# Fetching the second batch's first queries and keys earlier, and finishing the last tile in two halves

## The chip, the cores and the metric

One core of one Trainium2 chip. The time is the device time of one execution in microseconds (us). Every kernel was checked against the reference. A run counts as slow when it is over 1.5% above the fastest run of its kernel. All ratios compare fast runs alone; a median stands with all runs of its group.

## The reference

```python
# q, k, v: [4 batches, 8 heads, 768, 64]; mem_k, mem_v: [4, 8, 8, 64]; w1: [512, 2048]; w2: [2048, 512]
for c in range(768 // 32):                      # chunks of 32 queries, context 16 left and 8 right
    k_full = concat(mem_k, k[l_start:r_end])
    a = softmax(q[c] @ k_full.T / 8)
    attn[c] = a @ concat(mem_v, v[l_start:r_end])
x = attn.transpose(0, 2, 1, 3).reshape(4, 768, 512)
u = x + real(fft(fft(x, axis=1), axis=2))
un = (u - mean(u)) / sqrt(var(u) + 1e-6)
out = u + relu(un @ w1) @ w2
```

## The kernel before: the parts that matter

A batch is four "pairs" of heads: pairs 0 to 3 are the first batch, 4 to 7 the second, and so on. Each pair needs its query and key (loaded by GpSimd), its values (loaded by SyncE, then partly copied by GpSimd), transpositions, scores, exponentials, and the products with the values. Then come a batch's Fourier stage, its normalisation and the two large products (L669 with the first weights, L683 with the second).

```python
    def e_load_q(n):                            # L312; e_load_k (L317) alike
        b, pr = seq[n]
        nc.gpsimd.dma_start(qf[n % NS], q[b, 2 * pr:2 * pr + 2].rearrange(...))
    def e_overlap(n, hh):                       # L341, "the copies" of pair n
        v1 = va_at(n)[:, hh]
        nc.gpsimd.tensor_copy(v1[0:32, 1:NB, 0:D + 1], v1[96:128, 0:NT, 0:D + 1])
    # L439, the products with the values: 24 small matmuls in the trace for each half of a pair
    # L462, warm: matmuls of zeros that fill TensorE's holes
```

No engine runs in the order of the source. The kernel lists tasks, each with an engine, an estimated cost, what it comes after, and a rank; a small greedy planner walks through estimated time and places the first task that is ready, for every engine. "SPARE" gives margins, one row for each batch: the time by which what a task waits for must be done before the task may be placed. The order so found is fixed when the kernel is built.

```python
    SPARE = [(0.0, 0.0, 0.0), (1.5, 0.7, 2.0)] + [(1.0, 0.3, 0.5)] * (B - 2)
    def attention(n):
        b, pr = seq[n]
        behind1 = kept["ov"] if n == HP else None      # HP = 4: pair 4's query after the last copies of pair 3
        lq = add("POOL", 0.8, lambda: e_load_q(n), [behind1, kept.get("lk"), ...], take=("qf",), ...)
        lk = add("POOL", 0.8, lambda: e_load_k(n), [lq], take=("kf",), ...)
        mgp, mg, mgl = SPARE[b]
        ov = [add("POOL", 0.84, lambda hh=hh: e_overlap(n, hh), [lv[hh], calm], margin=mgl) for hh in range(2)]
        kept["ov"] = ov[-1]
        # ... transpositions, scores, exponentials, products with the values
    # ...
    with tc.manual_schedule():
        for plan.current in plan.order():
            plan.current["emit"]()
```

The softmax here doesn't subtract the row's maximum and nothing guards it: scores larger than these inputs give would overflow.

## Time and profile before

| | before |
|---|---|
| time, median of 3 (lowest to highest) | 308.03 us (307.89 to 308.85) |
| span of the profiled execution | 306.6 us, clock 0.999 |
| TensorE busy | 290.5 us, 95% |
| warm matmuls (zeros) | 170 |
| TensorE without work, 60 to 160 us | 6.3 us; 160 to 302 us: none |

TensorE is the bound, so time can only come from its holes and from the end. The profile's lines are in the prediction below.

### The profile page before, as it was taken

The page shows a single profiled execution, that of the slowest core. Times are in us where ns is not written, and L with a number is a line of the kernel's source. Part 1 is how long each engine was busy: PE and PEld are TensorE (multiplying, and loading weights), DVE is VectorE, ACT ScalarE, POOL GpSimd, SP SyncE. Part 2 cuts the span into 40 slices and gives each one's busy share as a digit, 9 for nine tenths or more (in the row PEclk, how much of TensorE's full clock was granted, in tenths as well). Part 3 has the DMA queues.
Part 4 walks back from the last instruction along what each step waited for, and adds up shares of the span by engine and source line. Part 5 has one row for each costly group of instructions (what it writes and reads, how often), then busy time and mean ns, then how long its engine had stood idle before and what let it go on. Part 6 is the DMA issues. An engine that isn't in the chain of part 4 may idle for free.

```text
span 306.6 us, 7853 instructions
## 1 busy us (share of the span) xinstructions
PE 290.5 (95%) x3335; PEld 193.2 (63%) x3335; DVE 177.6 (58%) x361; ACT 166.4 (54%) x297; POOL 72.7 (24%) x121
## 2 busy tenths in 40 slices
PE   8688999998999799997899999999999999999994
PEld 8577997666656476675566755767664554654641
DVE  7969968503525998699995989846911001001011
ACT  8967345887577556557475624641570450631710
POOL 7556837153336902223100020000010000000000
PEclk9999999999999999999999999999999999999999
DMA  6995999989996512323000010000000101102001
GB/s 81 151 174 116 190 199 197 198 140 154 206 194 119 95 40 61 94 57 92 2 0 2 2 71 35 2 34 34 36 0 34 72 0 68 36 0 90 15 34 68
DMA packets 42169, 24.49 MB, mean 80 GB/s; under 512 B 30359, under 2 KB 38551, under 8 KB 42135
## 3 DMA queue, kind: packets, MB, share of 16 engines
q0 software_dynamic: 9344, 10.49, 21.7%
q1 hardware_dynamic: 29335, 7.21, 13.0%
q10 hardware_dynamic: 3456, 6.29, 5.4%
q8 instruction: 26, 0.43, 0.6%
q14 instruction: 8, 0.07, 0.1%
HBM read 28.11 MB, written 6.29 MB: 112 GB/s over the span
## 4 chain that ended last, share of the span: by engine, by line
PE 84%; DVE 7%; ACT 6%; DMA 1%; issue 1%; POOL 0%; POOLq 0%; ACTq 0%
PE pc L683 27%; PE ph L669 26%; PE ps L513 9%; PE xa L439 6%; PE pm L548 5%; PE sc L384 2%; PE pm L612 2%; ACT e L427 2%; PE tp L648 1%; PE trq L348 1%; DMA qf<-in_q_dram 1%; PE trk L363 1%; PE warm L462 1%; ACT e L392 1%; ACT hT L676 1%; PE sc L417 1%
## 5 line engine op out<-in xcount | busy, mean ns | idle before, releaser
L676 ACT ACTIVATE hT<-ph 128x384 f16<-128x384 f32 x128 | 62.1, 491 | 60.0 <-PE ph L669 59.1
L669 PE MATMUL ph<-unT,w_sb 128*128 128x384 f16 x512 | 89.0, 326 | 3.4 <-ACT hT L676 1.7
L683 PE MATMUL pc<-w_sb,hT 128*128 128x512 f16 x384 | 89.0, 380 | 0.1
L669 PEld LDWEIGHTS <-w_sb 128*128 128x128 f16 x512 | 48.6, 98 | 35.5 <-issue 3.1
L689 DVE SCALAR_TENSOR_TENSOR osb<-pc,rstd,xsb 128x512 f32<-128x512 f32 x24 | 18.0, 750 | 75.5 <-PE pc L683 75.5
L683 PEld LDWEIGHTS <-hT 128*128 128x128 f16 x384 | 35.6, 98 | 39.3 <-issue 0.2
L341 POOL COPY va<-va 32x780 f32<-32x780 f32 x30 | 30.1, 1018 | 45.0 <-DMA va<-in_v_dram 43.9
L392 ACT ACTIVATE e<-sc,mbias 128x384 f32<-128x384 f32 x48 | 25.3, 582 | 9.1 <-PE sc L384 5.7
L439 PE MATMUL xa<-va,e 128*64 128x65 f32 x720 | 26.3, 225 | 0.0
L439 PEld LDWEIGHTS xa<-va,e 128*64 128x64 f32 x720 | 23.1, 137 | 4.1 <-issue 2.3
L642 ACT ACTIVATE un<-xsb,mu_s 128x512 f16<-128x512 f32 x18 | 13.0, 720 | 13.6 <-DVE mu_s L636 12.4
L660 POOL TENSOR_SCALAR rstd<-mu_s 128x6 f32<-128x6 f32 x4 | 1.0, 251 | 73.9 <-DVE mu_s L636 73.8
L450 DVE TENSOR_TENSOR xsb<-xa,zs 128x384 f32<-128x384 f32 x32 | 17.8, 557 | 1.1
L353 ACT COPY qT<-trq 128x768 bf16<-128x768 bf16 x14 | 11.2, 799 | 11.2 <-PE sc L384 11.2
L528 ACT CAST up<-ps 128x386 f16<-128x386 f32 x16 | 9.6, 603 | 13.5 <-PE ps L513 13.5
L635 DVE BATCH_NORM_STATS2 st<-xsb 128x6 f32<-128x512 f32 x24 | 16.5, 686 | 0.5
L449 DVE RECIPROCAL zs<-xa 128x6 f32<-128x6 f32 x32 | 6.1, 191 | 16.9 <-PE xa L439 16.5
L506 DVE TENSOR_TENSOR lo<-ff,hi 128x768 f16<-128x768 f32 x14 | 14.4, 1039 | 1.9 <-ACT hi L501 1.9
L501 ACT CAST hi<-ff 128x768 f16<-128x768 f32 x14 | 11.6, 830 | 7.1 <-DVE ff L594 4.7
L462 PE MATMUL warm<-zeros 128*128 128x128 bf16 x170 | 13.7, 245 | 1.0 <-DVE zero L249 1.0
L373 ACT COPY kTb<-trk 128x832 bf16<-128x832 bf16 x16 | 13.7, 858 | 1.4 <-PE sc L384 1.4
L629 DVE TENSOR_TENSOR xsb<-pm,xsb 128x512 f32<-128x512 f32 x18 | 12.1, 671 | 3.8 <-PE pm L548 3.8
(144 smaller groups left out, 400.9 us busy)
## 6 DMA issues: line engine op xcount, KB each, us to landing
out_dram<-osb ACTq DMA_DIRECT2D x24, 256.0 KB
va<-in_v_dram SPq DMA_DIRECT2D x30, 176.0 KB
w_sb<-in_moe_w_ch_dram POOLq DMA_DIRECT2D x8, 512.0 KB, 12.4
qf<-in_q_dram POOLq DMA_DIRECT2D x16, 192.0 KB, 5.3
kf_all<-in_k_dram POOLq DMA_DIRECT2D x16, 192.0 KB, 6.2
va<-in_mem_v_dram SPq DMA_DIRECT2D x30, 24.0 KB
va<-in_v_dram SPq DMA_DIRECT2D x15, 28.0 KB
last<-in_v_dram SPq DMA_DIRECT2D x2, 176.0 KB
```

Source lines behind the costliest of these rows:

```text
L341: nc.gpsimd.tensor_copy(v1[0:32, 1:NB, 0:D + 1], v1[96:128, 0:NT, 0:D + 1])
L392: nc.scalar.activation(e1[:, :, :, ts(half, 32)], sc[:, :, 0:6, ts(half, 32)], AFT.Exp, bias=mbias[:, half:half + 1], scale=1.0 / math.sqr ...
L439: nc.tensor.matmul(xa[64 * half:64 * half + 64, st, hh, 0:65], e1[:, hh, t6, :], v1[:, 6 * g + t6 + 1, 0:65], start=True, stop=True)
L450: nc.vector.tensor_tensor(xs[b][:, 3 * g:3 * g + 3, 2 * pr * D:(2 * pr + 2) * D] .rearrange("p s (h d) -> p s h d", h=2), xa[:, :, :, 0:D] ...
L462: nc.tensor.matmul(warm_of[0], zeros, zeros, start=True, stop=True)
L513: nc.tensor.matmul(out_[:, sp, :], part[:, ab, sp * 3 + st, c0:c1], tab[:, sp, st, :], start=(first and sp + st + i == 0), stop=(last and ...
L548: nc.tensor.matmul(pm[:, par, :], lhs, rhs[:, par, :], start=(im == 0), stop=(im == 3))
L635: nc.vector.bn_stats(st6, xs[b][:, kt, :])
L669: nc.tensor.matmul(ph[:, 0:384], w1_sb[:, dt, ts(ht, P)], unT_of[b][:, dt, sh * 384:(sh + 1) * 384], start=(dt == 0), stop=(dt == NDT - 1))
L676: nc.scalar.activation(hT_of[b, sh][:, ht, :], ph_of.pop((b, sh, ht))[:, 0:384], AFT.Relu, bias=0.0, scale=-1.0)
L683: nc.tensor.matmul(pc_of[b, sh, stl], hT_of[b, sh][:, ht, ts(stl, P)], w2_of[0][:, ht, :], start=(ht == 0), stop=(ht == NHT - 1))
L689: nc.vector.scalar_tensor_tensor(osb, pc_of.pop((b, sh, stl)), rstd_of[b][:, st:st + 1], xs[b][:, st, :], ALU.mult, ALU.add)
```

## The change

Intent: the queries and keys of pairs 4 and 5 are no longer fetched after the first batch's last copies, but between them, so that pair 4's transpositions and scores can fill holes of TensorE in the first batch's Fourier stage. At the end, the last tile's product is made in two halves of 256 columns, so that the last VectorE step and the last store are shorter. Pair 6's query, and so pair 7's, now comes behind the second weights.

```diff
     def attention(n):
         b, pr = seq[n]
-        behind1 = kept["ov"] if n == HP else None
+        behind1 = {HP: kept.get(("ov", 1)), HP + 1: kept.get(("ov", 2)),
+                   HP + 2: t_w2[-1] if n >= HP else None}.get(n)
 ...
-        kept["ov"] = ov[-1]
+        kept["ov"] = kept["ov", n] = ov[-1]
 ...
                 st = 3 * sh + stl
+                if (b, st) == (B - 1, NST - 1):
+                    for half in range(2):
+                        c2 = add("PE", 1.75, lambda half=half: e_ch2_half(half), ...)
+                        os_ = add("DVE", 0.42, lambda half=half: e_osb_half(half), [c2, rs], ...)
+                        add(("SP", "ACT")[half], 0.3, lambda half=half: e_out_half(half), [os_], ...)
+                    continue
```

More of the change, by code (lines that the diff above doesn't have):

```diff
@@ L684, in e_ch2, with e_ch2_half, e_osb_half, e_out_half @@
                              start=(ht == 0), stop=(ht == NHT - 1))
+    def e_ch2_half(half):
+        b, sh, stl = B - 1, 1, 2
+        pc_of[half] = bank([P, DM // 2], FP32, "pc_half")
+        for ht in range(NHT):
+            nc.tensor.matmul(pc_of[half], hT_of[b, sh][:, ht, ts(stl, P)],
+                             w2_of[0][:, ht, ts(half, DM // 2)],
+                             start=(ht == 0), stop=(ht == NHT - 1))
+    def e_osb_half(half):
+        b, st = B - 1, NST - 1
+        osb_of[half] = osb = fpool.tile([P, DM], FP32, tag="osb", bufs=3, name="osb")
+        cols = ts(half, DM // 2)
+        nc.vector.scalar_tensor_tensor(osb[:, 0:DM // 2], pc_of.pop(half),
+                                       rstd_of[b][:, st:st + 1], xs[b][:, st, cols],
+                                       ALU.mult, ALU.add)
+    def e_out_half(half):
+        eng = (nc.sync, nc.scalar)[half]
+        eng.dma_start(out[B - 1, ts(NST - 1, P), ts(half, DM // 2)],
+                      osb_of.pop(half)[:, 0:DM // 2])
     def e_osb(b, sh, stl):
@@ L1027, in mlp @@
                 st = 3 * sh + stl
+                if (b, st) == (B - 1, NST - 1):
+                    for half in range(2):
+                        c2 = add("PE", 1.75, lambda half=half: e_ch2_half(half),
+                                 [relu[-1], t_w2[-1], c2], take=("mlp",),
+                                 rank=MLPS + len(plan.tasks))
+                        os_ = add("DVE", 0.42, lambda half=half: e_osb_half(half), [c2, rs],
+                                  take=("osb",), give=(("mlp", c2),))
+                        add(("SP", "ACT")[half], 0.3, lambda half=half: e_out_half(half), [os_],
+                            give=("osb",), moved=0.5, rank=10 * MLPS)
+                    continue
                 for part in range(4):
```

## The prediction

> **What bounds the kernel now.** I read the page first (busy time, chain), then the table of windows, then the timeline around the two places that the diff touches, then the waits.
>
> ```profile
> PE 290.5 (95%) x3335; PEld 193.2 (63%) x3335; DVE 177.6 (58%) x361; ACT 166.4 (54%) x297; POOL 72.7 (24%) x121
> ...
> PE 84%; DVE 7%; ACT 6%; DMA 1%; issue 1%; POOL 0%; POOLq 0%; ACTq 0%
> ```
>
> TensorE is the bound: 84% of the chain that ended last. Its multiplications cannot shrink by this change, so the whole prize is the time in which TensorE waits or multiplies zeros to stay warm (L462). The table of windows says where it waits (span, then PE, PEld, DVE, ACT and POOL busy, clock, DMA share, GB/s):
>
> ```profile
> 20.00:30.00 10.00, 8.74 (x221) 7.60 (x221) 8.01 (x16) 6.99 (x12) 5.92 (x10) 1.00 0.62 115
> ...
> 60.00:70.00 10.00, 8.99 (x159) 6.05 (x156) 1.03 (x3) 9.10 (x18) 5.50 (x8) 1.00 0.95 150
> ...
> 100.00:110.00 10.00, 8.41 (x117) 5.44 (x113) 9.90 (x15) 6.13 (x11) 6.76 (x5) 1.00 0.36 65
> ...
> 140.00:150.00 10.00, 8.23 (x100) 5.34 (x99) 9.90 (x19) 7.78 (x14) 4.05 (x4) 1.00 0.25 66
> 150.00:160.00 10.00, 8.84 (x95) 6.63 (x94) 9.83 (x22) 5.75 (x11) 0.00 (x0) 1.00 0.01 2
> ```
>
> PE's missing time after 60 us is 1.0 (60 to 70), 0.2, 1.6 (100 to 110), 0.6 (130 to 140), 1.8 and 1.2 us: 6.3 us in all; from 160 to 302 us there is none. Where it misses most, VectorE is 98 to 99% busy. VectorE idles in 60 to 70 (1.03 us busy), and DMA has room in 20 to 30 (share 0.62, against 1.2 at 40 to 60). The lines of the timeline that the change turns on (start, duration, engine, line):
>
> ```profile
> 35.31 0.83 PE L462 MATMUL warm<-zeros 128*128 128x128 bf16 x12
> 38.00 0.50 PE L462 MATMUL warm<-zeros 128*128 128x128 bf16 x6
> 45.91 0.50 PE L462 MATMUL warm<-zeros 128*128 128x128 bf16 x6
> 65.43 0.35 PE L384 MATMUL sc<-qT,kTb 64*128 64x64 bf16 x12
> 43.72 0.63 POOL L317 DMA_DIRECT2D kf_all<-in_k_dram  x1 [2.02 <-DMA w_sb<-in_moe_w_ch_dram]
> 49.30 3.18 POOL L341 COPY va<-va 32x780 f32<-32x780 f32 x4
> 104.47 2.12 PE L669 MATMUL ph<-unT,w_sb 128*128 128x384 f16 x12 [1.59 <-DVE xsb L450]
> ```
>
> The warm matmuls fill holes during the first batch's Fourier stage; the second batch's first scores start only at 65.4 us, because its queries and keys queue behind the first weights (5.3 and 6.2 us median to landing, 15.6 and 14.9 at most). And the end:
>
> ```profile
> 302.33 0.75 DVE L689 SCALAR_TENSOR_TENSOR osb<-pc,rstd,xsb 128x512 f32<-128x512 f32 x1 [2.70 <-PE pc L683]
> 303.11 0.34 ACTq L693 DMA_DIRECT2D out_dram<-osb  x1
> ```
>
> **What the Trainium skill says.** "TensorE: Matmul & The Clock Gate", section "Wait — 56ns, not 53.3ns?", gives N / 2.4 GHz + about 2.5 ns between warm matmuls, 215.7 ns at N = 512. The trace agrees: 48 of L683 take 10.36 us in the chain, 215.8 ns each, and 48 of L548 (N = 256) take 5.24 us, 109.2 ns each. "DMA: Bandwidth & Descriptors", section "Anatomy of one DMA — SWDGE (gpsimd) path", says that a semaphore wait of a DMA happens on the issuing sequencer; the trace agrees, since GpSimd stands still 2.02 us before the key load at 43.72. "SBUF — State Buffer", section "SBUF: two separate sides", says that GpSimd and VectorE operations with two SBUF inputs lock each other out; the trace agrees: an addition of L481 takes 1.59 us beside the GpSimd copies at 99.7 us, 0.95 elsewhere.
>
> **The change part by part.** I compared the instruction orders of the two built kernels.
>
> (1) GpSimd now issues query and key of pair 4 (first of the second batch) after the copies of pair 1, and of pair 5 after those of pair 2: 2 x 1.4 us of issue (0.68 + 0.68 each) ahead of the last copies. Before, GpSimd is idle 2.3 us ahead of L585 at 27.43 us, waiting for VectorE. Working forward: copies of pair 1 end near 22.1, two issues to 23.5, copies of pair 2 (2.3 us in this trace) to 25.8, against 26.57 when TensorE's product needs them; two more issues to 27.2, when L585 can run at 27.4. It just fits. The bytes: four loads of 192 KB at some 195 GB/s are 4 us; the DMA shares of 22 to 29 us add up to about 3.3 of 7, so there is room, and I take up to 1 us of delay on the first weights.
>
> (2) TensorE: 18 warm matmuls disappear (170 become 152): 18 x 56 ns = **1.0 us**. In their place stand the 32 transpositions of pair 4 (0.34 + 0.37 us at the tightest rows of the chain) and its first 12 scores (0.35). Work leaves the bounded stretch and lands in a hole: -1.0 us on the path.
>
> (3) Scores and values of pairs 4 and 5 now come before and among the first L669 products instead of after 65 us. ScalarE and VectorE get their share of attention earlier, while VectorE idles, and value buffer 0 comes free some 15 us earlier. By my count of TensorE work the second batch's Fourier stage still begins after the same amount (93.1 before, 92.4 after), its columns come 4 us of work earlier and the third batch's rows 3 us later. So VectorE's crowded stretch is stretched a little. I expect about 1.5 of the 6.3 us of waits to go: the 1.0 of 60 to 70, and some of 140 to 152. This is the least certain term. **-1.5 us.**
>
> (4) A new wait. After the second weights GpSimd issues pairs 6, 7 and also 8 ahead of the copies (L341) of pair 4. Each GpSimd load waits for the one eight loads before it; for pair 8's key that is the second quarter of the second weights. Before, the first weights land near 43.7 us (the key load waited for them); a quarter is 512 KB, 2.7 us at 197 GB/s. So its landing is at 43.7 + 0 to 1 + 2 x 2.7 + 1 for value loads between, some 50.1 to 51.1; then 0.63 of issue and two copies of 0.84 end at 52.4 to 53.4. TensorE reaches the values of pair 4 at about 51.40 + 0.65 = 52.05, and the order puts them ahead of the first L669. **+0.8 us**, from 0 to 2.
>
> (5) The end. The last 16 matmuls of 512 become 2 x 16 of 256: 32 x 109.2 = 3.49 against 16 x 215.8 = 3.45 us, nothing. The last VectorE step halves: from 0.56 for 384 columns and 0.75 for 512 I estimate 0.38 for 256: -0.37. The last store falls from 256 to 128 KB; before, its bytes took about 0.65 us (0.96, 0.99, 0.58 of three quarter microseconds), so about -0.3; the first half leaves 1.75 us earlier on another queue. **-0.65 us.**
>
> Sum: -1.0 - 1.5 + 0.8 - 0.65 = -2.35, so 308.0 becomes about **305.7 us**.
>
> **The rivals.** (a) Nothing but the end moves: the weights, not queries and keys, pace the second batch. The DMA share is 1.2 from 44 to 64 us whatever the order, and the new wait (4) could take 2 us. For it: same bytes, full queues, and GpSimd's order of issue, so that copies stand behind weights. Against it: three holes are demonstrably filled by warm matmuls. Then 307 to 308.5.
> (b) VectorE becomes the bound in 94 to 160 us. It is 98 to 99% busy in four of those six windows, so earlier attention could free all waits there (6 us: 302) or none. For freeing: 26 us of VectorE idle in 60 to 100. Against: the count of TensorE work before the Fourier stage of the second batch is almost the same, so its rows cannot start much earlier. Then 303 to 304.
> (c) The early loads delay the first batch: values of pair 3 are issued at 21.2 to 24.1 us, beside query and key of pair 4, and the last copies need them at 27.7. If they land 2 us later, everything does. Against it: DMA is nearly idle at 26 to 28 us (shares 0.12 and 0.27). Then 308 to 310.
>
> **Range and chances.** The certain parts (2) and (5) are worth 1.65; (3) and (4) run from -3.5 to +1.5 together. That makes 303.3 to 308.0 as eight in ten. Two per cent is 6.2 us, about all of the waits after 60 us: faster 0.04. Slower by 6.2 needs rival (c) and a bad (4) together: 0.02. Within 2%: **0.94**.
>
> **What would show it.** Right: scores L384 first near 46 us instead of 65; 152 warm matmuls; PE idle below 0.5 us in 60 to 70; TensorE waiting up to 2 us for L341 or a product behind it near 52 us; the last store landing about 0.65 us sooner after the last matmul. Wrong: the first ps (L513, at 33.3 us) begins over 0.5 us later (rival c); or PE's idle time in 100 to 160 changes by over 2 us in either direction, which would say that (3), not (2), sets the result; or the L669 products of the first batch end as late in relation to the work done as before (rival a).

## The result, and the profile after

| | before | after |
|---|---|---|
| time, median (lowest to highest) | 308.21 us (307.89 to 308.85), 4 runs | 305.38 us over all 4 runs; 304.71 us (304.57 to 306.04) over the 3 fast ones; the fourth was slow, 309.99 at clock 0.983 |
| span of the profiled execution | 306.6 us | 304.2 us, clock 1.000 |
| warm matmuls | 170 | 152 |

The ratio is 0.9897, with a 95% interval of 0.9858 to 0.9935: within 2%. A ratio is the mean time of one kernel's fast runs over that of the other's of the same rounds, so not quite the ratio of the medians quoted. By this ratio and that of e1 (0.991) the gain is 2.8 to 3.2 us, where 2.35 was predicted: close. The profiled run was the slowest of the three fast ones. All outputs are right.

First the page of the changed kernel: busy time, then the chain, that is, the work that ended last, followed back step by step to what released it.

```profile
PE 290.3 (95%) x3333; PEld 193.2 (64%) x3333; DVE 179.2 (59%) x362; ACT 166.0 (55%) x297; POOL 73.1 (24%) x121
...
PE 75%; DVE 9%; DMA 7%; ACT 4%; POOL 2%; issue 2%; ACTq 0%; POOLq 0%; SPq 0%
```

TensorE's share of the chain fell from 84 to 75% and DMA's rose from 1 to 7%: a part of the path now runs through transfers. Now the table of windows after (span, then PE, PEld, DVE, ACT and POOL busy, clock, DMA share, GB/s; the DMA share is packet time over the time of 16 DMA engines, and can exceed 1):

```profile
20.00:30.00 10.00, 8.12 (x210) 7.02 (x205) 6.50 (x14) 6.24 (x11) 6.46 (x11) 1.00 1.06 163
...
60.00:70.00 10.00, 9.83 (x95) 5.84 (x93) 2.38 (x8) 8.81 (x20) 3.18 (x4) 1.00 0.99 166
...
100.00:110.00 10.00, 9.70 (x130) 5.74 (x128) 9.93 (x13) 7.37 (x15) 7.48 (x5) 1.00 0.48 97
110.00:120.00 10.00, 9.38 (x146) 6.96 (x143) 9.86 (x21) 6.03 (x10) 0.83 (x1) 1.00 0.30 70
...
140.00:150.00 10.00, 9.05 (x138) 5.91 (x137) 9.86 (x18) 6.96 (x14) 7.35 (x6) 1.00 0.39 89
150.00:160.00 10.00, 9.50 (x91) 6.50 (x90) 9.73 (x17) 5.88 (x12) 0.16 (x1) 1.00 0.00 0
```

From 60 to 70 TensorE's missing time fell from 1.0 to 0.2 us, as predicted; but from 50 to 60, where before none was missing, it is now 0.8. From 100 to 160 it fell from 5.1 us (the six windows of before) to 2.4, more than predicted. But from 20 to 30 TensorE lost 0.6 us of busy time, and the DMA share rose from 0.62 to 1.06. The timeline after, at the places that the prediction named:

```profile
26.96 1.23 PE L439 MATMUL xa<-va,e 128*64 128x65 f32 x36
...
29.29 0.57 PE L439 MATMUL xa<-va,e 128*64 128x65 f32 x12 [1.10 <-issue]
...
47.97 0.35 PE L384 MATMUL sc<-qT,kTb 64*128 64x64 bf16 x12
...
52.56 0.63 POOL L317 DMA_DIRECT2D kf_all<-in_k_dram  x1 [2.75 <-PE tp L648]
...
53.23 3.18 POOL L341 COPY va<-va 32x780 f32<-32x780 f32 x4
...
54.90 0.80 PE L439 MATMUL xa<-va,e 128*64 128x65 f32 x20 [0.44 <-POOL va L341]
```

The first scores of the second batch start at 47.97 instead of 65.43. Pair 4's copies stand behind pair 8's key load and end near 54.9, and TensorE waits for them. New and unforeseen is the line at 29.29: between two groups of the same products TensorE stands still, and the profile names no semaphore ("issue"). Two more places bear on the outcome. The first weights, which GpSimd issues behind the last copies of pair 3, leave 1.65 us later; before, then after:

```profile
29.24 2.18 POOL L867 DMA_DIRECT2D w_sb<-in_moe_w_ch_dram  x4
```

```profile
30.89 2.17 POOL L890 DMA_DIRECT2D w_sb<-in_moe_w_ch_dram  x4
```

And the head start of the second batch does not last. Each pair has two groups of 12 scores. Those of pair 4 start 17.5 us earlier, those of pair 5 only 3.6 (66.19 instead of 69.78), and those of pair 6 later than before; before, then after:

```profile
74.48 0.35 PE L384 MATMUL sc<-qT,kTb 64*128 64x64 bf16 x12
```

```profile
75.71 0.35 PE L384 MATMUL sc<-qT,kTb 64*128 64x64 bf16 x12
```

The end after:

```profile
297.12 3.66 PE L691 MATMUL pc_half<-w_sb,hT 128*128 128x256 f16 x32
...
300.81 0.48 DVE L699 SCALAR_TENSOR_TENSOR osb<-pc_half,rstd,xsb 128x256 f32<-128x256 f32 x1 [1.26 <-PE pc_half L691]
301.33 0.34 ACTq L705 DMA_DIRECT2D out_dram<-osb  x1
```

The last VectorE step shrank from 0.75 to 0.48 us. From the issue of the last store to the end of the wait for it on SyncE the trace has 1.73 us instead of 2.04.

**A curve of work.** Two kernels with different orders cannot be compared line by line. So I gave every TensorE matmul a fixed worth, its mean time per record (0.2158 us for L683, 0.1625 for L669, 0.1092 for L548, and so on; a warm matmul is worth 0), and read from each trace when a given amount of work had been started. The whole is 268.9 us of work in both kernels. What the small matmuls are worth is a matter of choice; with other worths for them (sums of 262 to 271 us) the times of a middle shift by up to 4 us, but its difference from before to after stays at 2.8 to 3.6. "Middle" below is the time from 50 to 146 us of work.

| work started | where it is | time before | time after | after - before |
|---|---|---|---|---|
| 10 us | first batch's attention | 26.35 | 26.73 | +0.4 |
| 15 us | its Fourier stage begins | 33.36 | 35.06 | +1.7 |
| 33 us | holes of that stage passed | 53.36 | 54.12 | +0.8 |
| 39 us | copies of pair 4 passed | 59.59 | 61.96 | +2.4 |
| 50 us | | 72.08 | 73.44 | +1.4 |
| 146 us | | 178.80 | 177.08 | -1.7 |
| all | end of the matmuls | 302.3 | 300.8 | -1.5 |
| | end of the span | 306.63 | 304.16 | -2.5 |

So the change loses 1.4 us by 50 us of work, gains 3.1 in the middle (106.7 against 103.6 us), and 0.8 after it.

### The profile page after: what moved, and what is told of

It is laid out like the page before. It is cut to its first block, busy times and chain, and to the rows that moved or that the text cites. A ratio compares the mean times of both kernels' runs of the same rounds, so it can differ in the third digit from the quotient of the medians.

```text
span 304.2 us, 7854 instructions
## 1 busy us (share of the span) xinstructions
PE 290.3 (95%) x3333; PEld 193.2 (64%) x3333; DVE 179.2 (59%) x362; ACT 166.0 (55%) x297; POOL 73.1 (24%) x121
## 4 chain that ended last, share of the span: by engine, by line
PE 75%; DVE 9%; DMA 7%; ACT 4%; POOL 2%; issue 2%; ACTq 0%; POOLq 0%; SPq 0%
PE pc L683 25%; PE ph L669 24%; PE xa L439 6%; PE pm L548 5%; DMA w_sb<-in_moe_w_ch_dram 5%; PE ps L513 4%; PE sc L384 2%; PE tp L648 2%; ACT e L427 2%; PE trq L348 2%; DMA qf<-in_q_dram 1%; PE trk L363 1%; PE pc_half L691 1%; DVE ff L490 1%; POOL va L341 1%
## 5 line engine op out<-in xcount | busy, mean ns | idle before, releaser
L669 PE MATMUL ph<-unT,w_sb 128*128 128x384 f16 x512 | 88.9, 326 | 2.0 <-ACT hT L676 1.7
L683 PE MATMUL pc<-w_sb,hT 128*128 128x512 f16 x368 | 85.7, 380 | 0.2 <-DVE osb L711 0.2
L669 PEld LDWEIGHTS <-w_sb 128*128 128x128 f16 x512 | 48.5, 98 | 34.5 <-issue 3.1
L711 DVE SCALAR_TENSOR_TENSOR osb<-pc,rstd,xsb 128x512 f32<-128x512 f32 x23 | 17.3, 751 | 74.8 <-PE pc L683 74.8
L683 PEld LDWEIGHTS <-hT 128*128 128x128 f16 x368 | 34.0, 98 | 37.1 <-issue 0.2
L341 POOL COPY va<-va 32x780 f32<-32x780 f32 x30 | 32.4, 1101 | 30.3 <-DMA va<-in_v_dram 30.1
L312 POOL DMA_DIRECT2D qf<-in_q_dram x16 | 10.5, 659 | 17.6 <-PE trq L348 13.1
L317 POOL DMA_DIRECT2D kf_all<-in_k_dram x16 | 10.2, 634 | 15.0 <-PE trk L363 5.2
L462 PE MATMUL warm<-zeros 128*128 128x128 bf16 x152 | 12.3, 246 | 1.0 <-DVE zero L249 1.0
```

What stands on the lines that cost most here:

```text
L669: nc.tensor.matmul(ph[:, 0:384], w1_sb[:, dt, ts(ht, P)], unT_of[b][:, dt, sh * 384:(sh + 1) * 384], start=(dt == 0), stop=(dt == NDT - 1))
L683: nc.tensor.matmul(pc_of[b, sh, stl], hT_of[b, sh][:, ht, ts(stl, P)], w2_of[0][:, ht, :], start=(ht == 0), stop=(ht == NHT - 1))
L711: nc.vector.scalar_tensor_tensor(osb, pc_of.pop((b, sh, stl)), rstd_of[b][:, st:st + 1], xs[b][:, st, :], ALU.mult, ALU.add)
```

## The experiments

Three questions: what is the stall at 28 us, what does the wait for pair 4's copies cost, and does the middle's gain come from the earlier attention, as step (3) of the prediction says, or is it only another order? The kernel before: medians 308.69 us (e1 to e4), 308.63 (e5 to e8) and 308.23 (e9 to e12), 11 runs each.

### e1: the change again

No edit.

> The changed kernel once more, unaltered. Its first profile lost 1.3 us at 28 us, in the middle of the values of pair 2, where TensorE waited for no semaphore; a 16 KB instruction fetch had started at 26.7 us, against 24.6 us before. Theory A (the fetch came late by chance of the queues): this profile shows no gap over 0.6 us between 20 and 29 us, and the fast runs fall into groups some 1.3 us apart (304.6 and 306.0 so far). Theory B (the early loads always delay the fetch): the gap of 1.0 to 1.5 us is there again and all fast runs lie within 0.5 us of each other, at about 305.5 or 306.

Measured: 306.36 us median of 7 runs, one of them slow (310.05); the 6 fast ones have 305.88 (304.84 to 307.56), ratio 0.991 [0.9879, 0.994]. The profiled run was the slow one (clock 0.972, and 0.50 from 20 to 30 us); its early stalls are not used. The gain is real, but the fast runs range over 2.7 us: neither the two groups of theory A nor the narrow one of theory B.

### e2: the end alone

```diff
-        behind1 = {HP: kept.get(("ov", 1)), HP + 1: kept.get(("ov", 2)),
-                   HP + 2: t_w2[-1] if n >= HP else None}.get(n)
+        behind1 = kept["ov"] if n == HP else None
```

> Only the last tile in two halves, with the loads as before. My step (5): 0.65 us less than before, 307.5 (ratio 0.998); the profiles of before and after differ by 0.84 us after the last matmul, so 0.6 to 0.9. Rival: the end is hidden or given back by the second store, ratio 1.000.

Measured: 307.40 us (306.99 to 308.64, 6 runs), ratio 0.9975 [0.9948, 1.0002], that is 0.8 us, with an interval that just reaches 1. In its trace the time from the end of the last matmul to the end of the span is 3.67 us instead of 4.34, and the middle is that of before (106.55). Step (5) holds.

### e3: the loads alone

```diff
-                if (b, st) == (B - 1, NST - 1):
+                if False:
```

> Only the early loads, the last tile as before. If the two parts add up, 0.8 us slower than the whole change (about 306.0 when the whole change is 305.2; ratio to before 0.992 to 0.994). Rival: the parts depend on each other, and this is as fast as the whole change or as slow as before.

Measured: 307.21 us (305.51 to 310.07, 6 runs), ratio 0.9967 [0.9926, 1.0009]. This is less than the 0.992 to 0.994 expected, and the interval holds 1, so the run times alone do not show a gain. In the trace the stall is there (1.05 us, at 27.5 us), the curve is 2.4 us late at 15 us of work, and the middle takes 103.6 us, as with the whole change. So loss and gain both belong to the loads. (Part of the 2.4 is the clock's, which was 0.50 from 32 to 34 us in this profile.) From the end of the last matmul to the end of the span this run has 4.02 us, the whole change 3.38: the halves are worth 0.65 us here too, and the other 0.3 by which the change's end is shorter than that of before comes with the loads; why is not known.

### e4: the early loads, with the old order of every other engine

The kernel before, with only GpSimd's four loads moved after planning; the instructions of TensorE, VectorE, ScalarE and SyncE are in the order of before.

```diff
+    placed = plan.order()
+    for n in (HP, HP + 1):      # query and key of pairs 4, 5 behind the copies of pairs 1, 2
+        move([kept["q", n], kept["k", n]], kept["ovs", n - HP + 1][-1])
```

> The kernel before with its order on TensorE, VectorE, ScalarE and SyncE unchanged to the instruction; only GpSimd issues queries and keys of pairs 4 and 5 as early as the change does. My theory (the gain is work moved into holes of TensorE, which needs the new order): no gain, ratio 0.998 to 1.004, 307.5 to 309.5. Rival (data that lands earlier lets everything behind it start earlier, whatever the order): at least half of the gain, ratio 0.995 or less.

Measured: 309.08 us (307.77 to 310.14, 6 runs), ratio 1.0016 [0.9985, 1.0046]. The timeline of e4 shows the stall again, as an idle time of 1.10 us:

```profile
26.92 1.23 PE L439 MATMUL xa<-va,e 128*64 128x65 f32 x36
...
29.24 0.57 PE L439 MATMUL xa<-va,e 128*64 128x65 f32 x12 [1.10 <-issue]
```

In the kernel before the same 48 products ran without a break:

```profile
26.57 1.58 PE L439 MATMUL xa<-va,e 128*64 128x65 f32 x48
```

The curve is 1.7 us late at 15 us of work and still 1.5 us late at the end; the middle takes 106.55 us, as in before. So the early bytes cost TensorE some 1.5 us in this trace, and what they were meant to gain needs a new order. (The run times show less, +0.5 us by the ratio, with an interval that holds 0; the profiled run was near the top of its group.)

**What the stall is.** The page lists a DMA queue for instructions:

```profile
q8 instruction: 26, 0.43, 0.6%
```

26 fetches of 16 KB. TensorE has 3333 + 3333 instructions in this trace, and 6666 / 256 is 26.04, so these are TensorE's instructions, 256 to a fetch. "Runtime: NRT & Kernel Launch", section "Instruction fetch mechanics", tells of such blocks of 16 KiB and calls their cost "mostly hidden". Whether it is hidden here follows the fetch's start. The table takes the third fetch of TensorE from the DMA records of each trace:

| run | fetch starts | TensorE stalls | resumes after the fetch's start |
|---|---|---|---|
| before | 24.62 | no | |
| e12 | 22.78 | no | |
| e7 | 24.82 | no | |
| e6 | 25.19 | no | |
| e5 | 25.46 | no | |
| e2 | 23.17 | no | |
| e8 | 23.74 | no | |
| e10 | 24.16 | no | |
| e9 | 25.14 | 0.49 | 2.86 |
| e11 | 26.00 | 0.55 | 2.44 |
| e3 | 25.89 | 1.05 (idle 0.82) | 2.7 |
| e4 | 26.52 | 1.32 (idle 1.10) | 2.7 |
| after | 26.68 | 1.32 (idle 1.10) | 2.6 |

(Here and in the text a stall of e3, e4 and after is the whole gap in the starts, and "idle" is what the timeline gives; for e9 and e11 it is the timeline's.) Each stall comes after the 36th of the 48 products. TensorE comes to this place at 27 to 29 us, and stalls where the fetch had not been under way for some 2.5 us. The fetch's packet itself took 0.88 to 1.17 us in the five runs with a stall, no longer than elsewhere (0.88 to 1.30 in the others), and TensorE resumed 1.56 to 1.69 us after the packet's end in all five; in the eight without a stall the packet had ended at least 1.74 us before TensorE came to the 37th product. No run holds the fetch apart from the rest, but this is as near as the traces come to showing that the stall is a wait for this fetch, and that what is late is the start of its packet. What the change does to the DMA queues there is plain in the windows of one microsecond, first before, then after:

```profile
27.00:28.00 1.00, 1.00 (x40) 1.00 (x36) 0.83 (x3) 0.64 (x1) 0.51 (x2) 1.00 0.27 62
```

```profile
27.00:28.00 1.00, 1.00 (x42) 1.00 (x37) 0.87 (x3) 1.00 (x2) 0.18 (x1) 1.00 1.34 194
28.00:29.00 1.00, 0.19 (x8) 0.10 (x3) 0.64 (x2) 0.02 (x1) 0.83 (x2) 1.00 1.26 198
```

The DMA share rose from 0.27 to 1.34, and in the next microsecond TensorE did 0.19 us of work. That the full queues delay the fetch's start is likely and not shown. The five stalls are among the six fast-run traces in which the loads of pairs 4 and 5 come at their early place, and none is among the seven others. But the sixth is e5: its DMA share was 1.17 to 1.30 from 25 to 29 us, nearly as full as with the change, and its fetch began just in time.

### e5: pair 4's copies ahead of pair 8's loads

The change, with one move after planning.

```diff
+    move(kept["ovs", HP], kept["k", HP + 3])     # behind pair 7's key, ahead of pair 8's loads
```

> The changed kernel with one move on GpSimd: the two copies of pair 4 go ahead of the loads of pair 8, all other engines keep their order. My step (4) puts the wait at 0.8 us (0 to 2): in the profile of the change TensorE stands 0.67 us at 54.2 us for the copies. Theory: that gap goes and the kernel gets 0.5 to 1.2 us faster than the changed kernel (ratio to before 0.986 to 0.989 where the changed kernel has 0.990). Rival: what is won there is lost at the next wait (pair 8's key later, or later waits on ScalarE), ratio 0.990.

Measured: 304.80 us (303.76 to 305.70, 6 runs), ratio 0.987 [0.9846, 0.9895]. The wait for L341 near 54 us is gone; from 33 to 39 us of work the curve loses 0.9 us against before, where the change loses 1.6. So the wait is worth some 0.7 us in the traces. This profile has no stall at 28 us, though nothing was changed there: that stall does not come in every run.

### e6: the loads of pairs 4 and 5 one pair of copies later

```diff
+    for n in (HP, HP + 1):
+        move([kept["q", n], kept["k", n]], kept["ovs", n - HP + 2][-1])
```

> The changed kernel with the loads of pair 4 behind the copies of pair 2, and of pair 5 behind those of pair 3: one pair of copies later each, other engines unchanged. Three profiles with the early loads stall TensorE at the same instruction, 1.05 to 1.3 us, 2.6 to 2.7 us after the start of an instruction fetch that begins 1.9 to 2.1 us later than before, in a stretch in which the DMA engines are now saturated (busy share 1.1 to 1.4 from 24.5 to 29.5 us). Theory: with the loads later the fetch starts near 24.6 us again, the stall at 28 us goes, and the kernel is 1.0 to 1.5 us faster than the changed one (ratio 0.985 to 0.987). Rival: the stall has nothing to do with the loads' position, or moves to the next fetch, and the weights, now 1.3 us later, delay the first products: ratio 0.990 or more.

Measured: 310.02 us (308.54 to 311.33, 6 runs), ratio 1.0033 [1.0002, 1.0064]. I had expected a gain: a miss. The stall at 28 us is indeed gone. But the waits and the timeline of e6 show where it went:

```profile
PE xa L439 <- POOL va L341: 4.6, 3, 3.7
```

```profile
55.52 0.63 POOL L317 DMA_DIRECT2D kf_all<-in_k_dram  x1 [2.76 <-DMA va<-in_v_dram]
56.19 3.18 POOL L341 COPY va<-va 32x780 f32<-32x780 f32 x4
57.07 0.34 PE L439 MATMUL xa<-va,e 128*64 128x65 f32 x4 [3.74 <-POOL va L341]
```

(The first line is engine, line, what it waited for: us in total, times, longest.) The whole chain of GpSimd's loads shifted, pair 8's key was issued at 55.52 instead of 52.56, and the copies behind it began 3.0 us later; TensorE waited 3.74 us for them. The line gives a load of values as the releaser of that key; but the load eight places before it, the second quarter of the second weights, landed at 54.96, and at 52.00 in the change: the key follows it by 0.56 us in both, as step (4) of the prediction has it. The wait of step (4) is where the prediction put it, and it is steep: in these traces GpSimd issues in order, so the copies pay for every load that stands waiting ahead of them.

### e7: both moves

The edits of e5 and e6 together.

> Both moves together. If the two losses are independent, the gains add: 1.5 to 2.5 us faster than the changed kernel, ratio to before 0.982 to 0.985. Rival: the later loads delay the second weights so that the copies wait for something else, and this is as fast as the better of the two.

Measured: 304.45 us over all 6 runs (5 fast ones, 302.60 to 304.93, median 304.30; one slow at 307.85), ratio 0.9841 [0.9813, 0.9868]. The timeline of e7 has the 48 products in one piece,

```profile
27.55 1.58 PE L439 MATMUL xa<-va,e 128*64 128x65 f32 x48
```

and no wait for the copies at 54 us. At 50 us of work it is 0.2 us ahead of before, where the change is 1.4 behind: the two repairs are worth 1.6 us together in the traces, and perhaps more, since the clock was 0.83 from 10 to 20 us in this profile (and in those of e5 and e6) and 1.00 in that of the change. By the ratios it is 0.9841 against 0.9897 and 0.991: 1.7 to 2.1 us, but from different calls.

### e8: the kernel before, its planner's margins nudged

No early load, no divided end.

```diff
-    SPARE = [(0.0, 0.0, 0.0), (1.5, 0.7, 2.0)] + [(1.0, 0.3, 0.5)] * (B - 2)
+    SPARE = [(0.0, 0.0, 0.0), (1.4, 0.65, 2.0)] + [(1.0, 0.3, 0.5)] * (B - 2)
```

> The kernel before with two planning margins of the second batch nudged (1.5 to 1.4, 0.7 to 0.65), which reshuffles the order on TensorE, VectorE and ScalarE from the second batch on and changes no load and no hole. My step (3) says that the waits between 95 and 155 us go because the second batch's attention is earlier; in the profiles that stretch gives 3.2 us. Theory: a mere reshuffle leaves this stretch within 1 us of before, ratio 0.997 to 1.003. Rival: the order of before is an unlucky draw there, and a reshuffle alone gets 2 us or more of it: ratio 0.994 or less (or it loses as much: 1.006 or more).

Measured: 306.21 us (305.96 to 307.66, 6 runs), ratio 0.992 [0.9898, 0.9941]. Moving two margins by 0.1 and 0.05 us gains 2.5 us, nearly what the whole change gained, and all of it in the middle (104.6 against 106.7 us). The windows of e8:

```profile
100.00:110.00 10.00, 8.79 (x121) 5.67 (x117) 9.90 (x15) 6.58 (x13) 6.51 (x5) 1.00 0.31 58
...
130.00:140.00 10.00, 8.16 (x164) 6.76 (x163) 9.62 (x22) 6.25 (x11) 1.67 (x2) 0.83 0.29 66
140.00:150.00 10.00, 9.90 (x112) 6.68 (x111) 9.90 (x18) 6.82 (x13) 4.58 (x4) 1.00 0.18 51
150.00:160.00 10.00, 10.00 (x127) 6.88 (x122) 7.75 (x19) 8.50 (x17) 0.00 (x0) 1.00 0.00 0
```

The holes of before at 140 to 160 (2.9 us) are nearly gone; the one at 130 to 140 grew from 0.6 to 1.8 us, at a clock of 0.83. The scores of pairs 4 to 6 start as in before (65.33, 69.69 and 74.41 us). So earlier attention is not needed for such a gain. Whether it makes it likelier, or even secures it, was still open.

### e9: the change, with the margins nudged in the same way

```diff
-    SPARE = [(0.0, 0.0, 0.0), (1.5, 0.7, 2.0)] + ...
+    SPARE = [(0.0, 0.0, 0.0), (1.4, 0.65, 2.0)] + ...
```

> The change with the two planning margins of the second batch nudged as in the run of the kernel before with the nudge (1.5 and 0.7 become 1.4 and 0.65), nothing else. Measured over the middle of the work, from 50 to 146 us of TensorE's useful work: before 106.7 us, before nudged 104.6, the change and its variants 103.5 to 104.1. If that middle is a draw of the scheduler's order, this one may land anywhere from 103.5 to 107, and the total from 304.5 to 308. If earlier attention is what frees the middle, it stays at 104.2 or less, and the total at 304.5 to 306.

Measured: 307.12 us over all 6 runs (5 fast ones, 305.45 to 309.83, median 307.07; one slow at 310.36), ratio 0.9966 [0.9925, 1.0007]. The middle took 105.3 us, over the 104.2 that "earlier attention" allowed. The clock in this profile fell to 0.91 and 0.92 from 100 to 120 us, so some of the excess can be the clock's.

### e10: the kernel before, the margins nudged up

```diff
+    SPARE = [(0.0, 0.0, 0.0), (1.6, 0.75, 2.0)] + ...
```

> The kernel before with the same two margins nudged the other way (1.6 and 0.75), nothing else: loads, holes and end as in before. If the middle is a draw: anywhere from 103.5 to 107 us, total 305.5 to 309. If earlier attention frees the middle: 104.6 or more, total 306 to 309. A middle under 104 without any early load would settle that the change's gain there needs no early attention.

Measured: 307.23 us (306.99 to 308.84, 6 runs), ratio 0.9971 [0.9951, 0.999]; middle 105.6 us at full clock. (The profiled run was the group's slowest, by a stall of 1.5 us near 40 us that precedes the middle.) In both theories' ranges.

### e11: the change, the margins nudged up

```diff
+    SPARE = [(0.0, 0.0, 0.0), (1.6, 0.75, 2.0)] + ...
```

> The change with the margins nudged up (1.6 and 0.75). Draw: middle 103.5 to 107 us, total 304.5 to 308. Earlier attention: middle 104.2 or less, total 304.5 to 306. If all three draws of the change are at or below 104.2 and two of three of before are above 104.5, early attention makes a good order likelier without being needed for it.

Measured: 308.44 us (307.28 to 309.71, 6 runs), ratio 1.0002 [0.9979, 1.0024]. This is the change, with early scores and the divided end, and it gains nothing. The windows of e11:

```profile
110.00:120.00 10.00, 8.54 (x126) 5.58 (x125) 9.90 (x18) 5.40 (x9) 1.93 (x2) 1.00 0.28 74
...
140.00:150.00 10.00, 8.42 (x114) 5.38 (x109) 9.79 (x19) 7.18 (x14) 4.38 (x5) 1.00 0.22 54
150.00:160.00 10.00, 9.10 (x89) 6.43 (x89) 9.93 (x17) 5.86 (x12) 0.85 (x1) 1.00 0.01 2
```

At a clock of 1.00 the middle took 107.1 us, as long as in the kernel before (with other worths for the small matmuls between 0.2 us less and 1.0 more), with holes beside a VectorE that is 98 to 99% busy. (1.2 us of the hole at 110 to 120 ends at 115.89 with no releaser that the profile names, so not all of it need be VectorE's.) This run falsifies "earlier attention frees the middle".

All orders together:

| instruction order | middle, us | ratio to before |
|---|---|---|
| before (before, e2, e4) | 106.7, 106.55, 106.55 | 1 |
| before, nudged down (e8) | 104.6 | 0.992 |
| before, nudged up (e10) | 105.6 | 0.9971 |
| the change (after, e1, e3, e5, e6, e7) | 103.6, 103.65, 103.6, 103.45, 103.6, 104.1 | 0.9897 and 0.991 |
| the change, nudged down (e9, e12) | 105.3, 105.3 | 0.9966 for e9 |
| the change, nudged up (e11) | 107.1 | 1.0002 |

Two things are seen. Within one order the middle repeats within 0.7 us, even where the run enters it 4 us late (e6): it belongs to the order, not to when loads land. Between orders it moves by some 3.5 us, and the change's three draws (mean 105.3) are no better than the three of before (mean 105.6). TensorE's idle time from 100 to 160 us, which needs no worths, agrees: 5.1, 3.2 and 3.9 us in before, e8 and e10, and 2.4, 3.1 and 4.7 in after, e9 and e11. The mean ratio of the change's three draws, with 0.9903 for the first, is 0.9957, that of the three of before 0.9964. Three draws are few; an advantage of less than some 2 us from earlier attention could hide in them. And the nudged margins are the second batch's own: that a margin which has nothing to do with that batch moves the middle as much was not tested.

### e12: both moves and the margins nudged

The edits of e7 and e9.

> The best version so far (loads of pairs 4 and 5 one pair of copies later, copies of pair 4 ahead of pair 8's loads: 304.45 us) with the margins nudged down. If the middle is a draw: 303.5 to 307.5. If both fixes are independent of the middle and early attention holds it down: 304 to 305. No stall of TensorE near 28 us and no wait for the copies at 54 us in either case.

Measured: 303.88 us (303.15 to 304.25, 4 runs), ratio 0.9851 [0.9832, 0.987]. The total lies in the draw's range and 0.1 us under the other, too close to tell them apart; the middle is that of e9 (105.3 us; the clock fell to 0.83 in one window of it). It does show the two repairs at work under another order: in the timeline the 48 products of pair 2 and the 24 of pair 4 run without a wait.

```profile
25.86 1.58 PE L439 MATMUL xa<-va,e 128*64 128x65 f32 x48
...
51.55 0.88 PE L439 MATMUL xa<-va,e 128*64 128x65 f32 x24
```

At 50 us of work it is 1.9 us ahead of before; 0.6 of that was there at 5 us of work already, before any early load. e7 and e12 are the best versions, 0.9841 and 0.9851, and cannot be told apart.

## Why the prediction was right, point by point

The time was right (305.7 against 305.38), but by luck, since its terms were not: in the traces steps (1) and (4) cost 2.5 us more than predicted, and step (3) gave 2.5 us more. All three signs that the prediction gave for being wrong came: the first ps started 1.70 us later (34.98 instead of 33.28), TensorE's idle time from 100 to 160 us changed by 2.8 us, and the last L669 product of the first batch came after as much work as before (81.2 us in both, with worths like the curve's).

| step | predicted | in the traces |
|---|---|---|
| (1) early loads beside the first batch | 0 (up to 1 us of delay on weights) | +1.7 up to 15 us of work |
| (2) holes filled | -1.0 | -0.9 |
| (4) wait for pair 4's copies | +0.8 | +1.6 between 33 and 39 us of work; 0.7 of it the wait itself (e5) |
| (3) fewer waits later | -1.5 | -1.0 up to 50 us of work, -3.1 in the middle, +0.2 after it |
| (5) the end | -0.65 | -1.0, of which 0.65 is the halves' (e2, e3) |
| sum | -2.35 | -2.5 |

- **(1) failed, by an effect that was not on my list.** I asked whether GpSimd had time for the issues, and it had: L585 ran at 27.82. I asked whether the bytes had room, and they had not: the DMA shares of 22 to 29 us add up to 7.1 of 7, where 3.3 had been used before (the sum was thin already: 3.7 left, and 4 us of bytes to add). So the last values of pair 3 came late, their copies waited 1.22 us, and the first weights were issued 1.65 us later and landed at 45.30 instead of 43.17, where I had allowed up to 1. And I did not ask what else rides on the DMA queues: TensorE's own instructions. The stall of 1.3 us accounts for most of the 1.7; 0.3 us was there at 5 us of work, before the early loads, and may be noise.
- **(2) held**: 18 warm matmuls fewer, 152 counted, and 0.9 us on the curve.
- **(3) failed in its reason.** Of the 1.0 us of 60 to 70, 0.8 went as predicted, but 0.8 us of new idle time stands at 50 to 60. The premise already fell short: the attention of pairs 4 and 5 came earlier, that of pairs 6 and 7 did not (scores of pair 6 at 75.71 instead of 74.48, of pair 7 at 83.26 instead of 80.51), so there was little left of the head start by the time the holes come. But the prediction's own test, a change of over 2 us in TensorE's idle time from 100 to 160, was met (5.1 to 2.4 us), so (3) and not (2) set the result, as it said that would mean. And e8, e10 and e11 show that this part is not the merit of earlier attention: the middle is a draw of the planner's order, between 103.5 and 107.1 us. The kernel before held the poorest of its three draws and the change the best of its three.
- **(4) held in its mechanism, and by luck in its size.** The copies stood behind pair 8's key load, that key followed the landing of the second quarter of the second weights (52.00, then 52.56), and TensorE waited for L341, 0.7 us between the starts of two products (0.44 idle). But both sides of this wait were later than worked out: the landing had been put at 50.1 to 51.1 and so the copies at 50.7 to 51.7, and they began at 53.23; TensorE was expected at 52.05 and came at 54.1. The rest of the 1.6 stays in e5 and lies around the first L669 products and the transpositions L648; no run isolates it. e6 shows that the wait grows one for one: the key came 3.0 us later, TensorE 0.8 us earlier, and the idle time there grew by 3.8, from 0.4 to 4.2.
- **(5) held.** VectorE's last step took 0.48 us, where I estimated 0.38: two points (0.75 for 512 columns, 0.48 for 256) put 0.21 us of it in a part that does not shrink. The store took 0.31 us less, as predicted. From the last matmul's end the halves are worth 0.65 us in both pairs of traces (4.34 and 3.67, 4.02 and 3.38).
- **Rival (a)** was wrong for pair 4, whose first scores moved to 47.97, and the holes were filled; for pairs 6 and 7 and for the end of the first batch's L669 it was right. Its doubt about (4) was fair. **Rival (b)** was the right place to doubt, since VectorE is full there in good and bad draws, but the deciding thing was the order, which it did not name. **Rival (c)** was half right: the first batch was late, by 1.7 us, and the values of pair 3 did land late, which delayed the weights. But TensorE's own lateness had another cause, as no product waited longer for these values: their copies waited 1.22 us (to 30.11), but their product starts only at 32.84.

A slip in the prediction's reading of the trace: L481 is a subtraction, and the long one starts at 98.97 us; that it took 1.59 us beside the copies of GpSimd stands.

What stays open: why the fetch began late in some of the runs with the early loads and not in e5, and whether it is delayed in the queue or issued late. Both need a record of the fetch's request, which the traces here do not give.

## What to carry to other kernels

Where a greedy planner sets the order, a change is judged against several draws of that order, made by nudging one of its margins a little, before and after; otherwise one compares two draws. A fetch moved into an idle stretch of the queues is not free: ask what else uses them there, instructions too, and what stands behind it on the issuing engine. And when a prediction's total comes out right, check its terms: here +2.5 and -2.5 us that were not predicted cancelled.

## What the Trainium skill lacked or had wrong

- "Runtime: NRT & Kernel Launch", section "Instruction fetch mechanics", calls the cost of a 16 KiB boundary "mostly hidden". With the DMA share at 1.2 to 1.4 it was not: TensorE stood still for 0.5 to 1.3 us in five traces, and resumed 2.4 to 2.9 us after the fetch began, 1.56 to 1.69 after its packet ended. The page has no duration for a fetch and no word on other traffic.
- "DMA: Bandwidth & Descriptors", section "Anatomy of one DMA — SWDGE (gpsimd) path", says that the wait of a DMA is done on the issuing sequencer. The runs agree, and add the price for compute behind it: in e6 GpSimd stood 2.76 us before a key load, its copies began 3.0 us later than in the change, and TensorE waited 3.74 us.
- No page that I read says how far an order alone moves a kernel bound by TensorE: six orders took 103.5 to 107.1 us for 96 us of work.
